# Shorter list of final waits, a first tile loaded in two halves, and two warming products fewer in a fused attention and feed-forward kernel

## The chip, the cores and the metric

The kernel runs on one core of one Trainium2 chip. The metric is the time of one execution on the device in microseconds (us), taken as the median over runs. Before the change three runs took 705.91, 705.12 and 705.55 us, so the median is 705.55 us.

The core's engines are TensorE (PE, matrix products), VectorE (DVE), ScalarE (ACT), GpSimd (POOL) and SyncE (SP). Each runs its own list of instructions in order, and semaphores make one list wait for another. In this kernel SP issues nearly all DMA transfers, POOL those that add to their destination.

## The reference, cut to what matters

All tensors are bf16. x is 2048 rows of 1024, wqkv is 1024 × 3072, wo 1024 × 1024, w_gate and w_up 1024 × 3584, w_down 3584 × 1024.

```
xn  = (x - mean(x)) / sqrt(var(x) + 1e-5)              # each row of 1024
q, k, v = split(xn @ wqkv)                             # 32 heads of 32
phi(t)  = where(t > 0, t + 1, exp(t)) + 1e-6
kv  = sum over rows of phi(k)^T v,  z = sum over rows of phi(k)   # per head
o   = (phi(q) @ kv) / (phi(q) . z + 1e-6)
s   = o @ wo
g   = silu( (silu(xn @ w_gate) * (xn @ w_up)) @ w_down )
out = x + s * g
```

The attention is linear: it needs no products between rows, but k and v of all 2048 rows must be there before any o can be made.

## The kernel before, in words

**A plan, then five lists.** The kernel first writes down every piece of work as an operation of a `Plan` (lines 31 to 216): its engine, what it reads and writes, an assumed duration, and, for a DMA, its size and semaphore. `op` (line 49) derives from reads and writes which operations must come before it. `schedule` (line 92) then fixes the order on each engine. It goes backwards through the operations and gives each a due time, the earliest that its followers allow, held to within `CLAMP` = 1000 us of PE's work so far, less its `urgent` (line 99). Then it goes forward: for PE it takes the first ready product in the order of writing, within a window of 10 operations; for any other engine it takes the ready operation with the smallest rank, due time less `boost` (line 144). The table `BOOST` (line 1730) gives boosts by the operation's number in the order of writing, so a number means another operation as soon as one is added or removed ahead of it. `emit` (line 187) turns the order into five lists of instructions and puts in a wait wherever an engine doesn't yet know that a predecessor is done. A chip executes the lists as they are; the plan's assumed times only set the order.

**What is computed when.** x is worked on in 16 tiles of 128 rows. `ln_tile` (line 734) normalises a tile: two `bn_stats` of half the columns each (lines 739 and 740), their aggregate (745), the variance plus epsilon (746), the power −0.5 on POOL (749), and for tiles 0 and 1 two `tensor_scalar` on DVE for half the columns each (755). `t_tile` (line 779) transposes the first four tiles on PE (line 237 is where the transposes are recorded) and copies them out of PSUM on ACT (804); later tiles are transposed by DMA. k and v of tiles 0 and 1 are made by plain products (`p_piece`, line 864), those of the other tiles by a scheme that needs seven products for a 2 × 2 block of tiles in place of eight. After that come q, gate, up, attention output and down projections, all in the seven-product scheme, in part nested twice, with intermediate results in DRAM scratch. Line 230 is where every matrix product is recorded, line 358 every ACT operation, line 368 every DVE addition or product of two tensors, line 371 every DMA of SP, line 222 every wait that needs an instruction of its own.

**The start.** PE first runs `NWARM` = 13 products of 128 × 512 on a zeroed tile (line 483 to 485), which nobody reads. Meanwhile SP issues the loads of lines 925 to 928. Each x tile is one DMA of 256 KB (`x_load`, 720), and the weights of k and v are eight blocks of 512 KB (`wkv_load`, 725). A block is called (w, j, k) here: w = 0 for k's weights and 1 for v's, j the half of the columns, k the half of the rows. k's products of tiles 0 and 1 need (0,0,0), (0,0,1), (0,1,0) and (0,1,1): the two with equal j make one result, four products for each block and tile. All loads of this list get `urgent` = 60 − 2n by their place in it (line 932), whatever they got before; the normalising products of tiles 0 and 1 get up to 100 (758), which their predecessors inherit through the due times. With its boosts SP issues x0, (0,1,0), x1, (0,0,0), (0,0,1), (0,1,1), and after those the rest. In `ln_tile` tile 1's first statistics also follow tile 0's variance and its second ones tile 0's second normalising product (741 to 744).

In the old table the entries 29 to 34 are the loads x0, x1, (0,1,0), (0,1,1), (0,0,0) and (0,0,1), and 41 and 42 are tile 0's two statistics.

**The end.** The output is made in four groups of 512 rows. The first three copy x to the output beforehand and add to it with POOL's accumulating DMAs (1593). The last group adds x on DVE and stores with plain DMAs of SP (1599): eight pieces of 128 × 512, except that the last piece is cut in three columns' ranges (`PIECES`, 1449), so there are ten stores, each with a semaphore of its own. After its last instruction SP waits for every DMA semaphore's final value, one by one in the order in which the semaphores were made (lines 1742 to 1744); consecutive waits are packed by the compiler where they can be.

Of the kernel before, what the change touches and what calls it, by code (L numbers as in the profile page):

```python
# [12 lines left out]
BF16 = mybir.dt.bfloat16  # L13
FP16 = mybir.dt.float16
KB = 1024
# [222 lines left out]
    return last  # L238


def build_kernel(nc, A_x, A_wqkv, A_wo, B_w_gate, B_w_up, B_w_down, out, WINDOW=10, NWARM=13, NPE=4, LEAD=16.0, CLAMP=1000.0, AHEAD=4.0):
    S, D, FF = 2048, 1024, 3584
    NT, KT, NG, NPAIR = 16, 8, 8, 14
    EPS_LN, EPS_PHI = 1e-5, 1e-6
# [1 line left out]
    xf = A_x.rearrange("b s d -> (b s) d")  # L246
# [7 lines left out]
    with ExitStack() as es:  # L254
# [20 lines left out]
        def named(*key):  # L275
            return Region([key])
# [11 lines left out]
        stats = TM.at(15 * KB + 256, 192, F32).rearrange("p (i h n) -> p i h n", h=2, n=6)  # L288
# [38 lines left out]
        def sem(name):  # L327
            return es.enter_context(nc.semaphore(name))

        esem = {k: sem("s_" + k) for k in Plan.ENGS}  # L330
        semn = {}

        def dsem(name):
            if name not in semn:
                semn[name] = sem("d_" + name)
            return semn[name]

        PL = Plan(WINDOW, LEAD, CLAMP, AHEAD)
# [18 lines left out]
        def act(reads, writes, o, i, func, src="ps", **kw):  # L357
            op = PL.op("act", reads, writes, lambda h: h.activation(o, i, func, **kw),  # L358
                       nel(o) / 1200.0 + (0.055 if src == "ps" else 0.095))
            if func in (ACT.Exp, ACT.Silu):  # L360
                op.tab = func
            return op

        def dve(reads, writes, fn, n, rate=0.96):
            return PL.op("dve", reads, writes, fn, n / (rate * 1000.0) + 0.07)
# [4 lines left out]
        def dma(reads, writes, o, i, s, nbytes, cow=None, after=None):  # L370
            return PL.op("sp", reads, writes, lambda h: h.dma_start(o, i), 0.08, sem=s, nbytes=nbytes, cow=cow,
                         after=after)
# [37 lines left out]
        def pool(reads, writes, fn, busy=0.3):  # L410
            return PL.op("pool", reads, writes, fn, busy)
# [308 lines left out]
        def x_load(i):  # L720
            s = x_ring.take()
            xslot[i] = s
            dma([], [s.r], s.ap(), xf[i * 128:(i + 1) * 128, :], dsem("x%d" % s.k), 256 * KB).urgent = 10.0

        def wkv_load(w, j, k):
            ap, r = kvblock(w, KB_OF[k, j])
# [5 lines left out]
        first_var = []  # L732

        def ln_tile(i):
            j = i % 4
            s = xslot[i]
            xa = s.ap()
            sA, sB, mvr, ver, rsr, nmr = (named(n, j) for n in ("sA", "sB", "mv", "ve", "rs", "nm"))
            o0 = dve([s.r], [sA], lambda h: h.bn_stats(stats[:, j, 0, :], xa[:, 0:512]), 512)
            o1 = dve([s.r], [sB], lambda h: h.bn_stats(stats[:, j, 1, :], xa[:, 512:1024]), 512)  # L740
            if i == 1:
                for o, p in ((o0, first_var[0]), (o1, first_var[-1])):
                    o.preds.add(p)
                    p.succs.append(o)
            dve([sA, sB, TM.reg(15 * KB + 256, 192)], [mvr], lambda h: h.bn_aggr(mv[:, j, :], stats[:, j, :, :]), 60)
            o0 = dve([mvr], [ver], lambda h: h.tensor_scalar(veps[:, j, :], mv[:, j, 1:2], EPS_LN, None, ALU.add), 60)
            if i == 0:
                first_var.append(o0)
            pool([ver, nh_r], [rsr], lambda h: h.tensor_tensor(rstd[:, j, :], veps[:, j, :], neg_half[:, :], ALU.pow), 0.56)
            o = xn_ring.take()  # L750
            xnslot[i] = o
            oa = o.ap(FP16)
            if i < 2:
                for c in (0, 512):
                    n = dve([s.r, mvr, rsr], [o.sub(2 * c, KB).r], lambda h, c=c: h.tensor_scalar(
                        oa[:, c:c + 512], xa[:, c:c + 512], mv[:, j, 0:1], rstd[:, j, :], ALU.subtract, ALU.mult),
                        512, 2.6)
                    n.urgent = 100.0 - c / 25 - 40 * i
                    if i == 0:
                        first_var.append(n)  # L760
            else:
                dve([mvr, rsr], [nmr], lambda h: h.scalar_tensor_tensor(
                    nmean[:, j, :], mv[:, j, 0:1], -1.0, rstd[:, j, :], ALU.mult, ALU.mult), 60)
                act([s.r, nmr, rsr], [o.r], oa, xa, ACT.Identity, "sb", bias=nmean[:, j, :],
                    scale=rstd[:, j, :]).busy = 1.13
# [159 lines left out]
        for n, (fn, args) in enumerate(((x_load, (0,)), (x_load, (1,)), (wkv_load, (0, 1, 0)), (wkv_load, (0, 1, 1)),  # L925
# [5 lines left out]
            for o in PL.ops[k:]:  # L931
                o.urgent = 60.0 - 2 * n
        ln_tile(0)
        t_tile(0)
        ln_tile(1)
        t_tile(1)
        p_piece(0, 0, 1)
# [3 lines left out]
        x_load(5)  # L941
        p_piece(1, 0, 0)
        ln_tile(2)
        p_piece(0, 1, 1)
        t_tile(2)
# [693 lines left out]
        sp = {}  # L1639
# [81 lines left out]
        for g, c in enumerate(G):  # L1721
# [5 lines left out]
        feed(None)  # L1727
        flush()

        BOOST = {1: 5058, 29: 18306, 30: 754, 31: 18202, 32: 872, 33: 880, 34: 881, 37: 3, 39: 68, 41: -2586,  # L1730
# [7 lines left out]
        for k, v in BOOST.items():  # L1738
            PL.ops[k].boost = v
        PL.schedule()  # L1740
        prog = PL.emit(esem)
        for s in semn.values():
            if id(s) in PL.count:
                prog["sp"].append(("w", s, PL.count[id(s)]))

        @block.tensor
        def _(h):
# [19 lines left out]
def bass_recurrent_scan__linear_attn_block__swiglu_ffn__prompt_kernel(  # L1767
    nc: bass.Bass,
    A_x: bass.AP,
    A_wqkv: bass.AP,  # L1770
    A_wo: bass.AP,
    B_x: bass.AP,
    B_w_gate: bass.AP,
    B_w_up: bass.AP,
    B_w_down: bass.AP,
    out: bass.AP,
):
    build_kernel(nc, A_x, A_wqkv, A_wo, B_w_gate, B_w_up, B_w_down, out)
# [28 lines left out]
```

## Time and profile before

| | |
|---|---|
| median of three runs | 705.55 us (705.12 to 705.91) |
| the profiled execution | 704.51 us |
| its span, first to last instruction | 702.7 us |
| mean granted TensorE clock | 0.998 |
| PE busy | 694.8 us, 4436 products and transposes |
| DVE, ACT, POOL busy | 610.7, 424.7, 68.4 us |
| DMA | 103.68 MB, mean 148 GB/s |

The profile is of one execution. Its times count from the first instruction. The execution took 1.81 us more than its span, which lies around the instructions. A busy time is a sum of an engine's durations; PE's weight loads (PEld) go beside its products. In a timeline or chain a row gives start, length, engine, line of the kernel, operation, what is written and read, shapes, the number of instructions taken together, and in brackets the idle time of the engine before it and what ended it. `SPq` is SP's queue of instructions, whose DMA issues aren't counted as busy.

### The profile page before, as it was taken

How to read it: one execution, taken by the hardware profiler on the slowest of the kernel's cores; microseconds unless marked ns; L12 is line 12 of the kernel's file. 1: busy time of each engine (PE TensorE's matmuls, PEld its weight loads, DVE VectorE, ACT ScalarE, POOL GpSimd, SP SyncE). 2: the span in 40 equal slices, each digit the busy share in tenths (PEclk: the TensorE clock that was granted, in tenths of full speed). 3: DMA queues.
4: the chain of work that ended last, by engine and by line, in shares of the span. 5: the costliest groups of instructions: out<-in, count | busy, mean ns of one | idle time of the engine just before them, and what ended most of it. 6: DMA issues, size and time to landing. Idle time of an engine off the chain costs nothing.

```text
span 702.7 us, 11996 instructions
## 1 busy us (share of the span) xinstructions
PE 694.8 (99%) x4436; PEld 421.4 (60%) x4436; DVE 610.7 (87%) x1391; ACT 424.7 (60%) x848; POOL 68.4 (10%) x87
## 2 busy tenths in 40 slices
PE   8999999999999999999999999999999999999996
PEld 3544445555555566666666666666665448687784
DVE  6999998667999799898999999888879998768685
ACT  4877645867978967868866567775763113232222
POOL 2111000001100011020110110001101211111010
PEclk9999999999999999999999999999999999999999
DMA  9434213126612376584670486766627875666672
GB/s 313 106 83 106 54 60 121 61 90 145 155 61 69 117 195 169 174 236 101 166 194 1 106 242 198 242 218 165 165 81 225 192 182 176 155 165 156 207 180 69
DMA packets 96107, 103.68 MB, mean 148 GB/s; under 512 B 18256, under 2 KB 91344, under 8 KB 95952
## 3 DMA queue, kind: packets, MB, share of 16 engines
q1 hardware_dynamic: 84976, 92.43, 41.9%
q0 software_dynamic: 11072, 10.49, 11.9%
q8 instruction: 35, 0.57, 0.3%
q14 instruction: 24, 0.20, 0.1%
HBM read 65.54 MB, written 37.36 MB: 146 GB/s over the span
## 4 chain that ended last, share of the span: by engine, by line
PE 99%; ACT 0%; POOL 0%; DVE 0%; issue 0%; POOLq 0%
PE ps L230 99%; PE ps L237 0%; ACT X L358 0%; DVE W L368 0%; POOL TM L415 0%; ACT W L358 0%; POOL TM L414 0%; POOLq L1792 0%
## 5 line engine op out<-in xcount | busy, mean ns | idle before, releaser
L358 ACT ACTIVATE TM<-ps 128x512 f32<-128x512 f32 (+2 forms) x341 | 169.0, 528 | 50.5 <-PE ps L230 45.6
L368 DVE TENSOR_TENSOR ps<-ps,TM 128x256 f32<-128x256 f32 (+1 forms) x322 | 157.7, 509 | 40.2 <-PE ps L230 35.8
L230 PE MATMUL ps<-X,W 128*128 128x512 f16 (+1 forms) x896 | 190.4, 340 | 0.0
L230 PE MATMUL ps<-P,W 128*128 128x512 f16 (+1 forms) x896 | 188.9, 338 | 0.0
L358 ACT ACTIVATE H<-ps 128x512 f16<-128x512 f32 (+1 forms) x181 | 106.3, 601 | 55.9 <-PE ps L230 54.9
L230 PEld LDWEIGHTS ps<-X,W 128*128 128x128 f16 (+1 forms) x896 | 87.5, 98 | 59.5 <-DVE W L368 0.2
L230 PEld LDWEIGHTS ps<-P,W 128*128 128x128 f16 (+1 forms) x896 | 87.6, 98 | 58.4 <-DVE ps L368 0.2
L358 ACT ACTIVATE ps<-ps 128x256 f32<-128x256 f32 (+2 forms) x149 | 63.5, 426 | 72.5 <-PE ps L230 70.9
L230 PE MATMUL ps<-H,X 128*128 128x512 bf16 (+4 forms) x556 | 104.8, 336 | 0.5 <-ACT X L358 0.5
L368 DVE TENSOR_TENSOR H<-H 128x1024 f16<-128x1024 f16 (+5 forms) x150 | 87.1, 598 | 10.6 <-ACT H L358 8.4
L368 DVE TENSOR_TENSOR W<-W 128x256 f16<-128x256 bf16 (+6 forms) x256 | 89.1, 388 | 5.1 <-PE ps L230 2.9
L230 PE MATMUL ps<-W 128*128 128x256 f16 x512 | 90.0, 273 | 0.0
L368 DVE TENSOR_TENSOR TM<-ps,TM 128x512 f32<-128x512 f32 x99 | 67.8, 686 | 12.5 <-PE ps L230 11.5
L230 PEld LDWEIGHTS ps<-H,X 128*128 128x128 f16 x556 | 52.8, 98 | 41.6 <-ACT X L358 0.6
L375 POOL DMA_DIRECT2D h_scratch<-H x28 | 33.7, 1283 | 437.4 <-DVE H L368 197.0
L230 PEld LDWEIGHTS ps<-W 128*128 128x128 f16 (+1 forms) x512 | 50.0, 98 | 27.3 <-ACT TM L358 0.6
L230 PE MATMUL ps<-H,W 128*128 128x512 f16 (+2 forms) x280 | 63.6, 358 | 0.0
L230 PE MATMUL ps<-H 128*128 128x256 f16 (+4 forms) x432 | 60.9, 273 | 0.0
L230 PE MATMUL ps<-W,H 128*128 128x256 f16 (+1 forms) x314 | 53.5, 305 | 0.0
L358 ACT ACTIVATE H<-TM 128x512 f16<-128x512 f32 x61 | 38.3, 631 | 15.6 <-DVE TM L368 15.0
L230 PEld LDWEIGHTS ps<-H 128*128 128x128 f16 (+1 forms) x432 | 38.3, 98 | 14.6 <-ACT H L358 0.2
L368 DVE TENSOR_TENSOR H<-ps,TM 128x512 f16<-128x512 f32 (+1 forms) x59 | 40.3, 685 | 2.7 <-PE ps L230 2.5
(92 smaller groups left out, 552.1 us busy)
## 6 DMA issues: line engine op xcount, KB each, us to landing
h_scratch<-H SPq DMA_DIRECT2D x70, 256.0 KB, 3.2
X<-h_scratch SPq DMA_DIRECT2D x15, 896.0 KB, 5.2
W<-in_B_w_gate_dram SPq DMA_DIRECT2D x7, 1024.0 KB, 5.4
W<-in_B_w_up_dram SPq DMA_DIRECT2D x7, 1024.0 KB, 6.1
h_scratch<-H POOLq DMA_DIRECT2D x28, 256.0 KB, 5.7
H<-in_B_w_down_dram SPq DMA_DIRECT2D x8, 896.0 KB, 6.7
W<-in_A_x_dram SPq DMA_DIRECT2D x16, 256.0 KB, 3.1
H<-in_A_wqkv_dram SPq DMA_DIRECT2D x8, 512.0 KB, 7.9
```

Of the source, the lines that this page charges most:

```text
L230: last = h.matmul(o, l, r, start=st, stop=sp, skip_group_check=True)
L358: op = PL.op("act", reads, writes, lambda h: h.activation(o, i, func, **kw), nel(o) / 1200.0 + (0.055 if src == "ps" else 0.095))
L368: return dve(reads, writes, lambda h: h.tensor_tensor(o, a, b, op), nel(o), 1.92 if fast else 0.96)
L375: return PL.op("pool", reads, writes, lambda h: h.dma_start(o, i, accum_op=ALU.add), 1.0, sem=s, nbytes=2 * nbytes)
```

## The change

Four things are edited. The number of warming products goes from 13 to 11. Tile 0's load is cut into two halves of 512 columns each, 128 KB; SP issues the first and ACT the second, with a new semaphore, and the statistics of a half then depend on that half alone; tile 0's second statistics follow its first. Both statistics of tile 1 now follow tile 0's second normalising product. And the final waits are only for DMAs that have no successor in the plan, with the last value of each such semaphore. The table of boosts is replaced; since two warming operations go and one load is added, an operation after the loads has a number one lower than before.

```diff
-def build_kernel(..., WINDOW=10, NWARM=13, ...):
+def build_kernel(..., WINDOW=10, NWARM=11, ...):
...
         def x_load(i):
             s = x_ring.take()
             xslot[i] = s
-            dma([], [s.r], s.ap(), xf[i * 128:(i + 1) * 128, :], dsem("x%d" % s.k), 256 * KB).urgent = 10.0
+            rows = xf[i * 128:(i + 1) * 128, :]
+            if i == 0:
+                dma([], [s.sub(0, KB).r], s.ap(BF16, 0, KB), rows[:, 0:512], dsem("x0"), 128 * KB)
+                PL.op("act", [], [s.sub(KB, KB).r], lambda h: h.dma_start(s.ap(BF16, KB, KB), rows[:, 512:1024]), 0.5,
+                      sem=dsem("xh"), nbytes=128 * KB)
+                return
+            dma([], [s.r], s.ap(), rows, dsem("x%d" % s.k), 256 * KB).urgent = 10.0
...
-            o0 = dve([s.r], [sA], lambda h: h.bn_stats(stats[:, j, 0, :], xa[:, 0:512]), 512)
-            o1 = dve([s.r], [sB], lambda h: h.bn_stats(stats[:, j, 1, :], xa[:, 512:1024]), 512)
+            o0 = dve([s.sub(0, KB).r], [sA], lambda h: h.bn_stats(stats[:, j, 0, :], xa[:, 0:512]), 512)
+            o1 = dve([s.sub(KB, KB).r], [sB], lambda h: h.bn_stats(stats[:, j, 1, :], xa[:, 512:1024]), 512)
+            if i == 0:
+                o1.preds.add(o0)
+                o0.succs.append(o1)
             if i == 1:
-                for o, p in ((o0, first_var[0]), (o1, first_var[-1])):
+                for o, p in ((o0, first_var[-1]), (o1, first_var[-1])):
...
-        BOOST = {1: 5058, 29: 18306, 30: 754, 31: 18202, 32: 872, 33: 880, 34: 881, 37: 3, 39: 68, 41: -2586,
-                 42: 6519, 46: 4544, 49: 3050, 51: 459, 60: 181, 78: 407, 80: 3, 104: 60, 117: 570, 123: 103, 142: 3,
+        BOOST = {1: 724, 27: 73363, 32: 9572, 33: 881, 44: 20, 45: 85, 46: 120, 48: 1646, 71: 80, 99: 150, 110: 224,
+                 112: 20, 122: 3053, 123: 20, 143: 6, 151: 8, 154: 8, 258: 20, 950: 3, 954: 60, 971: 8, 1931: 20,
...
         prog = PL.emit(esem)
-        for s in semn.values():
-            if id(s) in PL.count:
-                prog["sp"].append(("w", s, PL.count[id(s)]))
+        ends = {}
+        for o in PL.order:
+            if o.sem is not None and not o.succs:
+                ends.pop(id(o.sem), None)
+                ends[id(o.sem)] = o.ev
+        for s, _, val, _ in ends.values():
+            prog["sp"].append(("w", s, val))
```

More of the change, by code (lines that the diff above doesn't have):

```diff
@@ L238, in _tr_group, with build_kernel @@
     return last
-def build_kernel(nc, A_x, A_wqkv, A_wo, B_w_gate, B_w_up, B_w_down, out, WINDOW=10, NWARM=13, NPE=4, LEAD=16.0, CLAMP=1000.0, AHEAD=4.0):
+def build_kernel(nc, A_x, A_wqkv, A_wo, B_w_gate, B_w_up, B_w_down, out, WINDOW=10, NWARM=11, NPE=4, LEAD=16.0, CLAMP=1000.0, AHEAD=4.0):
     S, D, FF = 2048, 1024, 3584
```

10 rows, old and new, of the table BOOST are left out of this document.

## Prediction

> **What bounds the kernel now.** I read the page first: the span and how much of it TensorE (PE) works.
>
> ```profile
> span 702.7 us, 11996 instructions
> PE 694.8 (99%) x4436; PEld 421.4 (60%) x4436; DVE 610.7 (87%) x1391; ACT 424.7 (60%) x848; POOL 68.4 (10%) x87
> ```
>
> PE is busy for all but 7.9 us. A mean does not say where those lie, so the second view is the busy time by stretches (columns: stretch and length, then busy us and count of PE, PE weight loads, DVE, ACT, POOL, then granted clock, DMA share, GB/s).
>
> ```profile
> 1.40:7.00 5.60, 5.57 (x16) 2.09 (x17) 2.87 (x7) 0.68 (x1) 2.92 (x14) 1.00 0.93 303
> 7.00:11.10 4.10, 3.63 (x29) 1.84 (x26) 1.81 (x6) 1.20 (x3) 0.55 (x1) 1.00 1.10 363
> 11.10:100.00 88.90, 88.90 (x496) 43.71 (x495) 85.95 (x213) 64.31 (x101) 10.17 (x14) 1.00 0.42 107
> 100.00:600.00 500.00, 500.00 (x3157) 302.17 (x3155) 445.72 (x1017) 331.56 (x689) 41.11 (x37) 1.00 0.55 149
> 600.00:696.80 96.80, 96.74 (x748) 71.58 (x745) 73.53 (x148) 26.07 (x57) 12.99 (x16) 1.00 0.61 166
> ```
>
> From 11.1 to 696.8 us PE is busy 685.64 of 685.70 us: the middle is bound by PE alone and has nothing to give. The diff removes no product there, so a new order of the side engines can only keep this or spoil it. What can be won lies before 11.1 us and after 696.8 us.
>
> The third view is SyncE's (SP's) own instructions after 696 us: its stores of the output (durations, first and last start), how long the last store takes to land (KB, us), and the event-semaphore instructions of line 222, before and after 700.5 us.
>
> ```profile
> L371 SPq DMA_DIRECT2D out_dram<-W x4: 332/431/600, 696.0 to 697.9; - x4
> ```
> ```profile
> out_dram<-W SPq DMA_DIRECT2D x2, 32.0 KB, 1.5
> ```
> ```profile
> L222 SPq EVENT_SEMAPHORE  x34: 17/28/28, 698.4 to 700.4; - x34
> ...
> L222 SPq EVENT_SEMAPHORE  x25: 27/28/28, 700.8 to 702.2; - x25
> ```
>
> The last store is issued at 697.9 and lands 1.5 us later, at 699.4. Yet SP goes on until 702.2, through 59 instructions (34 and 25) that wait for the semaphores of all DMAs. Each takes 28 ns but they start 0.06 us apart (34 in 2.0 us), with one pause of 0.4 us between 700.4 and 700.8. From 699.4 on nothing is outstanding: SP only walks through a list. **The end is bound by the length of that list, not by the last store.**
>
> The fourth view is the timeline of the start.
>
> ```profile
> 0.80 1.28 ACT L358 ACT_TABLE_LOAD   x1 [0.80 <-PEq L1792]
> ...
> 1.26 0.42 SPq L371 DMA_DIRECT2D H<-in_A_wqkv_dram  x1
> ...
> 1.43 5.59 PE L230 MATMUL ps<-TM 128*128 128x512 f16 x13 [1.43 <-POOL TM L415]
> ...
> 1.73 0.51 SPq L371 DMA_DIRECT2D W<-in_A_x_dram  x1
> ...
> 2.27 2.29 SPq L371 DMA_DIRECT2D H<-in_A_wqkv_dram  x4
> ...
> 3.37 0.69 DVE L739 BATCH_NORM_STATS2 TM<-W 128x6 f32<-128x512 bf16 x1 [2.18 <-DMA W<-in_A_x_dram]
> ...
> 5.78 0.73 DVE L755 TENSOR_SCALAR W<-W,mv,rstd 128x512 f16<-128x512 bf16 x2 [0.69 <-POOL rstd L749]
> ...
> 6.43 0.69 DVE L739 BATCH_NORM_STATS2 TM<-W 128x6 f32<-128x512 bf16 x1
> ...
> 6.85 0.61 PE L237 MATMUL ps<-TM,W 128*128 128x128 f16 x8
> ...
> 7.93 2.80 PE L230 MATMUL ps<-H,X 128*128 128x512 bf16 x12 [0.47 <-ACT X L358]
> ...
> 8.82 0.73 DVE L755 TENSOR_SCALAR W<-W,mv,rstd 128x512 f16<-128x512 bf16 x2 [0.67 <-POOL rstd L749]
> ...
> 11.11 1.29 DVE L368 TENSOR_TENSOR H<-H 128x1024 f16<-128x1024 bf16 x2 [1.56 <-DMA H<-in_A_wqkv_dram]
> ...
> 11.13 8.81 PE L230 MATMUL ps<-H,X 128*128 128x512 bf16 x40
> ```
>
> The first half of tile 0 is normalised by about 6.15 (5.78 and half of 0.73), but its transposes start at 6.85, when the 13th warming product is through: here the warming is the bound, by 0.7 us. And at 11.11 a DVE operation, at 11.13 PE, start as the fourth weight block arrives: **there the bound is DMA arrival**, which the row of 7.0 to 11.1 us supports with 363 GB/s.
>
> **The change part by part.** *End waits.* The list of 59 instructions shrinks to the semaphores of DMAs that no later operation follows. By the code these are the ten stores of the last row group, each with a semaphore of its own; accumulating stores are followed by the next writer of their buffer. Ten waits are at most ten instructions, 0.6 us from 698.35, so SP stands ready by 699.0 and waits for the last store at 699.4. Behind the last wait the old kernel needed 0.45 us to its end (702.25 to 702.7); the new one then ends at about 699.4 + 0.05 + 0.45 = 699.9. The saving is 2.8 us. Bounds: 2.4 if the pause of 0.4 us comes back, 2.9 if the last wait is passed at once. What is late next is the last store itself, issued and landing as before.
>
> *Eleven products.* 13 took 5.42 us (1.43 to 6.85), 0.42 each, so two fewer give 0.83: PE is free at 6.0. The transposes can then start at 6.0 to 6.2, set by whichever is later, warming or normalising: 0.65 to 0.83 us earlier than now. Whether that reaches the end is decided by the weights, below.
>
> *Two halves.* No row of this trace shows a DMA issued by ACT. An issue of x1 took SP 0.51 us; on ACT it comes ahead of the table load of 1.28 us, which carries the line of the first ACTIVATE, and both are done by about 2.6, long before ACT's first work near 6.5. So it costs nothing there. If instead the table load goes first, the second half is issued at 2.08, 1.28 late, and lands near 4.6; its statistics, now possible from 4.06 (3.37 + 0.69), would start 0.55 late and the transposes near 6.7, about where they are now. At best half the bytes at 363 GB/s land 0.36 us sooner. I take no gain and no loss: the warming holds the transposes until 6.0 anyway.
>
> *Statistics of tile 1 behind both normalisings of tile 0.* In the trace they already come behind them (6.43 after 5.78 + 0.73 with its overlap). DVE has only tile 1's own chain behind the wait. Nothing, as long as tile 1 arrives later than 6.5; the next part says that it does.
>
> *The order of the loads.* This is the part the short list does not name. SP takes loads by due time less boost. The old boosts gave x0, (0,1,0), x1, (0,0,0), (0,0,1), (0,1,1). With two products fewer and one load more, every later index is one lower; the new entries at 27, 32 and 33 are x0's first half, (0,0,0) and (0,0,1). Due times are clamped to within about 1000, so 73363 and 9572 decide outright, and 881 nearly so; of the others x1 is due before the blocks, since it inherits the urgency of the normalising. The new order is x0, (0,0,0), (0,0,1), x1, (0,1,0), (0,1,1). How long a place in that queue takes is shown by the issues of the second, third and fourth load (KB, us to landing):
>
> ```profile
> H<-in_A_wqkv_dram SPq DMA_DIRECT2D x1, 512.0 KB, 4.2
> ```
> ```profile
> W<-in_A_x_dram SPq DMA_DIRECT2D x1, 256.0 KB, 4.4
> ```
> ```profile
> H<-in_A_wqkv_dram SPq DMA_DIRECT2D x1, 512.0 KB, 5.8
> ```
>
> With the issue times, 768 KB have landed at 1.26 + 4.2 = 5.5, 1024 KB at 1.73 + 4.4 = 6.1, 1536 KB at 2.27 + 5.8 = 8.1, and 2560 KB at 11.1, which puts 2048 KB at 9.6. The sum of bytes stays, so the new kernel has (0,0,0) at 5.5, (0,0,1) at about 7.1, **x1 at 8.1 in place of 6.1**, (0,1,0) at 9.6 and (0,1,1) at 11.1. Now PE's work: transposes at 6.1, first products 1.08 later as now (6.85 to 7.93) at 7.2, eight of them at 0.22 (8.81 over 40) to 8.95, with two blocks. Then it waits 0.65 us for (0,1,0), and does four more until 10.5. Tile 1's transposes need its normalising, which begins 2.39 us after its statistics (6.43 to 8.82), at 10.5; the halves are ready at 10.9 and 11.25. They end near 11.45, and the last four products of tile 0 near 12.3. The old kernel has done the same work, eight transposes twice and sixteen products, by 11.13 + 4 × 0.22 = 12.0. So **the 0.7 us won at the transposes are given back as waits for weights and for x1**. Bounds: 0.3 to 0.5 lost if x1 lands as late as its place says and PE holds its last products for it; 0.2 gained if two queues fill the engines sooner. I take a loss of 0.15.
>
> *A shorter warming and the clock.* The 13 products ran at 0.42 us, the later ones of the same shape at 0.22: TensorE ran at half pace until nearly 6.85, though the granted clock stands at 1.00 in the rows above. If it opens at the same moment, near 6.7, the new transposes partly run at half pace: up to 0.45 us, hidden by the 0.65 us that PE then waits for (0,1,0). The Trainium skill, "TensorE: Matmul & The Clock Gate", section "What's actually happening", holds that the gate opens after a free-running window of about 3.4 us in which PE was busy. The trace agrees: its 5.3 us of half pace are more than one such window and less than two. By that rule fewer warming products, followed by PE's waits, can miss a window, which would open the gate near 10.1; an estimate for that is 703.5 us.
>
> *Sum*, against the profiled execution's 704.51 us (span 702.7 and 1.8 around it): −2.8 + 0.15 + 0 = −2.65, or 701.9. The median of the runs shown, 705.55, is 1.04 above that execution; with the same difference I forecast **702.9 us**.
>
> **The rivals.** *First, the start gains as well.* Then x1 lands well before its place and PE does not wait at 9 us: up to 0.6 us more, 702.1. Against it is the arrival of (0,1,1) at 11.1 in both orders, with too little work ready before it. *Second, the new order leaves a hole in the middle.* Some seventy boosts change. For it: DVE is busy 85.95 of 88.90 us before 100 us, so an operation that goes first there delays another. Against it: PE waited nowhere for 685 us. One late buffer costs about 1 us (an operation of DVE or two): 703.9. *Third, the gate stays half shut.* Place: PE's work after 6.1. In the trace half pace lasted from 1.43 to about 6.7, 5.3 us, without an idle stretch. If the idle moments after the eleventh product start that anew, it lasts until 11.4: half of the work in 5.3 − 0.6 us (the wait for ACT) is lost, 2.35, less about 1.1 hidden in the waits near 9 and 11, so 1.2: 704.1. If the wait near 11 starts it once more, it lasts until 16.3, costs (10.2 − 0.6) / 2 − 1.1 = 3.7 and gives 706.6, slower than before. That side begins where the loss passes 2.65, with an opening later than about 6.1 + 0.6 + 2 × 3.75 = 14.2 us. Against it: the old kernel's transposes end near 7.3 (eight, a quarter of 0.22 each), PE then waits 0.6 us until 7.93, and that did not bring half pace back. *Fourth, the end does not shrink:* more DMAs than the ten count as last. With half the list left SP ends at 698.35 + 1.9 + 0.45 = 700.7, 2.0 sooner, which gives 703.7; with all of it, 705.7.
>
> **How the numbers follow.** Forecast 0.62; start gains 0.13; hole in the middle 0.12; gate late once 0.06, twice 0.03; end not shrunk 0.04. 0.2% of 705.55 is 1.4 us, about what a measurement of this kernel can tell from no change: faster means below 704.14, slower above 706.96. All of the first two count as faster, three quarters of the hole, two thirds of the gate late once and half and more of the fourth: 0.91 faster, 0.06 same, 0.03 slower. The range goes from 702.0 (start gains) to 704.1 (a hole, or a gate late once), and the runs shown differ by 0.4 either way, which lies within it around the forecast.
>
> **What would show it.** Right: at most ten event-semaphore instructions on SP after the last store, and an end 0.5 us after it lands; transposes near 6.1; a wait of PE near 9 us and one near 11, and PE dense from about 11.4. Wrong: PE idle between 12 and 696 us (second rival), products of 0.42 us after 7.5 (third), or sixteen products of tile 0 done well before 12.0 (first).

## The result, and the profile after

The kernel before ran in 705.25 us (median of six runs, 704.91 to 705.91), the changed one in 702.86 us (six runs, 702.68 to 703.69). The ratio is 0.9968, with a 95% interval of 0.9956 to 0.998. The forecast was 702.9 us. The total holds. Of the sum's two terms that were not zero one, the final waits, was right to a tenth; the other, the start's loss, was more than four times too small; and in the profiled execution a cost came on top that the sum did not have.

That execution took 703.48 us, 0.62 above the median of its kernel, where the one of before lay 0.74 below its own. So the two profiles differ by 1.0 us only, the medians by 2.4. The page after shows the span and PE:

```profile
span 701.7 us, 11926 instructions
PE 692.4 (99%) x4413; PEld 420.9 (60%) x4434; DVE 610.7 (87%) x1391; ACT 424.4 (60%) x848; POOL 67.9 (10%) x87
```

Here 4413 of PE's products were recorded; 4434 weight loads stand beside them, so some 20 records are missing, and PE's sums below are short by about as much. The stretches of the changed kernel (columns as before):

```profile
7.00:12.30 5.30, 3.53 (x25) 1.68 (x25) 2.89 (x7) 1.11 (x3) 0.55 (x1) 1.00 1.08 361
12.30:100.00 87.70, 87.23 (x483) 43.27 (x490) 83.94 (x210) 63.77 (x100) 9.67 (x14) 1.00 0.44 104
100.00:600.00 500.00, 499.53 (x3144) 301.69 (x3151) 445.83 (x1018) 331.72 (x688) 40.51 (x36) 1.00 0.55 149
```

From 12.3 us on PE is as dense as it was: the gaps of 0.47 us stand where there are 7 records fewer than weight loads. In the 5.3 us before, it works 3.53. The timeline of the start shows why (start, length, engine, and in brackets the idle time before and what ended it):

```profile
0.81 0.40 ACTq L726 DMA_DIRECT2D W<-in_A_x_dram  x1
...
1.43 3.94 PE L230 MATMUL ps<-TM 128*128 128x512 f16 x11 [1.43 <-POOL TM L415]
2.27 0.50 SPq L371 DMA_DIRECT2D W<-in_A_x_dram  x1
...
3.56 0.69 DVE L745 BATCH_NORM_STATS2 TM<-W 128x6 f32<-128x512 bf16 x1 [2.36 <-DMA W<-in_A_x_dram]
...
6.58 0.72 PE L237 MATMUL ps<-TM,W 128*128 128x128 f16 x8 [1.20 <-DVE W L764]
7.67 1.04 PE L230 MATMUL ps<-H,X 128*128 128x512 bf16 x4 [0.37 <-ACT X L358]
8.67 0.69 DVE L745 BATCH_NORM_STATS2 TM<-W 128x6 f32<-128x512 bf16 x1 [1.82 <-DMA W<-in_A_x_dram]
10.11 1.90 PE L230 MATMUL ps<-H,X 128*128 128x512 bf16 x8 [1.41 <-DMA H<-in_A_wqkv_dram]
11.06 0.73 DVE L764 TENSOR_SCALAR W<-W,mv,rstd 128x512 f16<-128x512 bf16 x2 [0.67 <-POOL rstd L758]
...
11.85 0.61 PE L237 MATMUL ps<-TM,W 128*128 128x128 f16 x8
...
12.30 1.03 PE L230 MATMUL ps<-H,X 128*128 128x512 bf16 x4
```

The warming ends at 5.37 and now PE waits 1.2 us for DVE: tile 0's normalising has become the bound of the transposes, at 6.58, and no longer the warming. After four products PE waits 1.41 us for block (0,1,0); tile 1's statistics begin at 8.67, where they began at 6.43 before; its transposes begin at 11.85; and tile 0's last four products begin at 12.30.

The end shows SP's issues of the output (durations in ns: least, median, most; first and last start), its last semaphore instructions, and how long the last stores took to land:

```profile
L371 SPq DMA_DIRECT2D out_dram<-W x5: 332/430/1292, 696.4 to 699.7; - x5
```
```profile
L222 SPq EVENT_SEMAPHORE  x5: 17/28/28, 700.2 to 701.3; - x5
```
```profile
out_dram<-W SPq DMA_DIRECT2D x2, 32.0 KB, 1.5
```

59 instructions have become five. The last one starts at 701.3, when the last store (issued at 699.7, 1.5 us to landing) is there, and the span ends about 0.5 us later. Nothing is walked through after the landing. But one issue took 1292 ns, where the longest took 600 before.

### The profile page after: what moved, and what is told of

Read it like the earlier page. It is cut to its first block, busy times and chain, and to the rows that moved or that the text cites. A ratio compares the mean times of both kernels' runs of the same rounds, so it can differ in the third digit from the quotient of the medians.

```text
span 701.7 us, 11926 instructions
## 1 busy us (share of the span) xinstructions
PE 692.4 (99%) x4413; PEld 420.9 (60%) x4434; DVE 610.7 (87%) x1391; ACT 424.4 (60%) x848; POOL 67.9 (10%) x87
## 4 chain that ended last, share of the span: by engine, by line
PE 97%; DMA 1%; DVE 0%; ACT 0%; SPq 0%; issue 0%
PE ps L230 97%; DMA H<-in_A_wqkv_dram 1%; SPq L371 0%; PE ps L237 0%; DVE H L844 0%; ACT TM L358 0%; ACT H L358 0%; DVE TM L843 0%; ACT ps L358 0%; DVE W L368 0%; ACT W L358 0%; DVE nmean L771 0%
## 5 line engine op out<-in xcount | busy, mean ns | idle before, releaser
L230 PE MATMUL ps<-H,X 128*128 128x512 bf16 (+4 forms) x545 | 102.6, 335 | 2.4 <-DMA H<-in_A_wqkv_dram 1.4
```

What stands on the lines that cost most here:

```text
L230: last = h.matmul(o, l, r, start=st, stop=sp, skip_group_check=True)
```

## The experiments

Each kernel ran five times or more, beside the kernel before, and each has a profile. Medians of such small changes overlap, so two readings of the profile are compared as well. They split a time at two points that every kernel has: the landing of the fourth block of k's weights, (0,1,1) in both orders, and the end of the last two DVE additions, which make the last piece of output. Between them lies nearly all the work; after the second lies the end. In the kernel before, and then in the changed one, these additions are

```profile
697.08 0.48 DVE L368 TENSOR_TENSOR W<-W 128x128 f16<-128x128 f16 x2 [0.22 <-ACT W L358]
```
```profile
698.24 0.49 DVE L368 TENSOR_TENSOR W<-W 128x128 f16<-128x128 f16 x2 [0.22 <-ACT W L358]
```

With the landing at 11.09 the first gives 697.56 − 11.09 = 686.47 us of work. In the changed kernel the block is issued at about 3.3 and lands 8.3 later, at 11.57:

```profile
H<-in_A_wqkv_dram SPq DMA_DIRECT2D x1, 512.0 KB, 8.3
```

which gives 698.73 − 11.57 = 687.16: **0.69 more**. Over the kernels with the old loads the reading repeats to 0.04 us. The end takes 702.7 − 697.56 = 5.1 us before, 701.7 − 698.73 = 3.0 after.

### The new final waits alone: end_only

The theory was the prediction's: the end gives about 2.8, the start next to nothing. The rival was that the start gave part of it, or took part of it back.

```diff
(kernel before)
-        for s in semn.values():
-            if id(s) in PL.count:
-                prog["sp"].append(("w", s, PL.count[id(s)]))
+        ends = {}
+        for o in PL.order:
+            if o.sem is not None and not o.succs:
+                ends.pop(id(o.sem), None)
+                ends[id(o.sem)] = o.ev
+        for s, _, val, _ in ends.values():
+            prog["sp"].append(("w", s, val))
```

> The kernel before with the new final waits alone; plan and every other instruction are as before. My theory (the end gives about 2.8 us and the start takes some back): 2.8 us less than before, about 702.4 us, that is below the changed kernel. Rival (the end gives only what the changed kernel's median shows, 2.4 us, and the start changes nothing): 702.85 us. Second rival (SP is late with the last store, so the list was partly hidden): 2.2 us less, 703.1 us.

Measured: 702.49 us (702.11 to 703.24) against 705.18 before in the same session, ratio 0.9958 [0.9945, 0.9971]. The one edit gives 2.7 us, no less than the whole change. Its profile, SP's instructions and then DVE's last additions:

```profile
L371 SPq DMA_DIRECT2D out_dram<-W x5: 332/430/1122, 695.8 to 699.0; - x5
```
```profile
L222 SPq EVENT_SEMAPHORE  x5: 17/28/28, 699.5 to 700.6; - x5
```
```profile
697.72 0.49 DVE L368 TENSOR_TENSOR W<-W 128x128 f16<-128x128 f16 x2 [0.22 <-ACT W L358]
```

The list of the emitted instructions is the old one up to the final waits, and the work from the landing (11.70) to the additions takes 698.21 − 11.70 = 686.51, as before. One thing is not as before: an issue of 1122 ns.

### The changed kernel with the old final waits: start_only

```diff
(changed kernel)
-        ends = {}
-        for o in PL.order:
-            if o.sem is not None and not o.succs:
-                ends.pop(id(o.sem), None)
-                ends[id(o.sem)] = o.ev
-        for s, _, val, _ in ends.values():
-            prog["sp"].append(("w", s, val))
+        for s in semn.values():
+            if id(s) in PL.count:
+                prog["sp"].append(("w", s, PL.count[id(s)]))
```

> The changed kernel with the old list of final waits: halves, eleven warming products, the new order of tile 1's statistics and the new boosts without the new end. My theory: slower than before by what the start loses, 0.4 to 1.2 us, 705.7 to 706.5 us, with PE idle for about 1.6 us before the products that need block (0,1,0). Rival (the start changes nothing): 705.3 us. Rival (the start gains): below 704.8 us.

Measured: 706.22 us (twelve runs, 704.55 to 708.38) against 705.18, ratio 1.0015 [1.0005, 1.0026]. All edits of the start together lose 1.0 us, between 0.4 and 1.8. The runs lie far apart: nine from 704.55 to 706.55, three from 708.13 to 708.38. The three have a mean granted clock of 0.996, the nine of 0.997 to 0.999. The profiled execution, 708.15 us, is one of the three. Its semaphore instructions at the end, and PE's timeline of the start:

```profile
L222 SPq EVENT_SEMAPHORE  x59: 27/28/28, 702.0 to 706.0; - x59
```
```profile
7.80 1.04 PE L230 MATMUL ps<-H,X 128*128 128x512 bf16 x4 [0.37 <-ACT X L358]
11.12 3.50 PE L230 MATMUL ps<-H,X 128*128 128x512 bf16 x8 [2.28 <-DMA H<-in_A_wqkv_dram]
14.46 0.61 PE L237 MATMUL ps<-TM,W 128*128 128x128 f16 x8
14.90 7.07 PE L230 MATMUL ps<-H,X 128*128 128x512 bf16 x32
```

Eight products take 3.50 us here, 1.90 in the changed kernel's profile, although the 32 after them take 0.22 each. The granted clock of that stretch (the third number from the end of the row) says the same, and DVE's last additions give the price:

```profile
10.98:14.39 3.41, 3.27 (x8) 1.19 (x9) 2.71 (x7) 0.00 (x0) 0.55 (x1) 0.50 1.10 355
```
```profile
700.85 0.48 DVE L368 TENSOR_TENSOR W<-W 128x128 f16<-128x128 f16 x2 [0.22 <-ACT W L358]
```

Half pace came back after a wait of 2.28 us, which is **the third rival's mechanism in an execution**. Its price is 3.50 − 1.90 = 1.6 us; the work from the landing (12.56) to the end of the additions (701.33) is 688.77, 1.6 above the changed kernel's 687.16. The changed kernel has the same start, so it is open to this as well; its six runs, up to 703.69 us, show no such step. The Trainium skill, "TensorE: Matmul & The Clock Gate", section "What's actually happening", puts the return to half pace after at least one idle window of some 3.4 us; here PE had no such pause, only 2.28 us, with little work (four products) in the 3.4 us before 11.1. In this execution a shorter pause was enough.

The 59 instructions run from 702.0 to 706.0; the last store lands at 703.1, so some 2.9 us of the list lie behind it. From the last additions to the end of the span, less the duration of the issue of the 64 KB store, it is 5.13 − 0.60 = 4.53 us before and 5.08 − 0.51 = 4.57 here, but 3.02 − 1.29 = 1.73 after and 2.85 − 1.12 = 1.73 in end_only: the list was worth 2.8 us in both starts.

### The products of the block that comes first: pe_swap

PE's list in the changed kernel has the four products of (0,1,0) ahead of those of (0,0,1), although (0,0,1) lands 2.2 us sooner. This kernel exchanges them.

```diff
(changed kernel)
         PL.schedule()
+        # the four products of (0,0,1) right before the four of (0,1,0)
+        o = PL.ops[75]
+        PL.order.remove(o)
+        PL.order.insert(PL.order.index(PL.ops[62]), o)
```

> The changed kernel with one change in PE's list: the four products of block (0,0,1) go ahead of the four of block (0,1,0); all loads stay where they are. If PE's order alone makes the wait at 8.5 us, the wait shrinks to 0.7 us and the kernel gains 0.35 us, until tile 1's transposes (its normalising ends near 11.8 us) hold PE: 702.5 us. If the late second tile is the only bound, nothing is gained: 702.86 us.

Measured: 703.22 us (701.61 to 704.5) against 705.18, ratio 0.9968 [0.9956, 0.998]. No gain. PE's timeline shows what is then in the way, the second fence how long the fourth block took, and the third DVE's last additions:

```profile
11.14 1.04 PE L230 MATMUL ps<-H,X 128*128 128x512 bf16 x4 [1.11 <-DMA H<-in_A_wqkv_dram]
12.58 0.72 PE L237 MATMUL ps<-TM,W 128*128 128x128 f16 x8 [0.40 <-DVE W L764]
13.13 7.07 PE L230 MATMUL ps<-H,X 128*128 128x512 bf16 x32
```
```profile
H<-in_A_wqkv_dram SPq DMA_DIRECT2D x1, 512.0 KB, 9.3
```
```profile
699.19 0.49 DVE L368 TENSOR_TENSOR W<-W 128x128 f16<-128x128 f16 x2 [0.22 <-ACT W L358]
```

Now PE has eight products behind it when (0,1,0) comes, as the prediction had assumed; it does four more and waits 0.40 us for DVE's normalising of tile 1. From the landing (12.58) to the end of the additions (699.67) it is 687.09 us, nearly what the changed kernel takes. So PE's list alone does not make the loss: with it out of the way, the late x1 holds PE almost as long. In the changed kernel the two end together, PE's eight products by 11.85 and tile 1's normalising at 11.06 + 0.73 = 11.79; what the list alone would cost no run shows.

### The first loads and products in the old order: old_start_order, early_loads_old

Both keep the halves, the eleven products, the order of the statistics and the new waits, and put the first loads of SP (x1, (0,1,0)) and PE's first products back in the old order. The first of them also puts a block of v's weights ahead of tile 2 of x, as in the kernel before.

```diff
(changed kernel; ahead(n, m) moves operation n right before m in PL.order)
         PL.schedule()
+        for n, m in ((30, 32), (29, 32), (38, 34), (62, 74)):    # old_start_order
+        for n, m in ((30, 32), (29, 32), (62, 74)):              # early_loads_old
+            ahead(n, m)
```

> The changed kernel with the loads of x1 and of the six weight blocks in the order of the kernel before, and PE's first three groups of products in the old order too; halves, eleven warming products, final waits and all later work as in the changed kernel. If the new order of loads is what the start pays for, PE reaches the products of (0,1,1) near 11.2 us and the kernel gains 0.7 to 1.1 us on the changed one: 701.8 to 702.2 us. If the halves or the shorter warming are to blame, it gains less than 0.3 us: 702.6 to 702.9 us.

> The changed kernel with x1 and the four k blocks in the old order of loads and PE's two first groups of products swapped to fit; unlike the earlier try, the third x tile keeps the place that the changed kernel gives it, ahead of v's first blocks. Theory (the new order of loads is what the start pays for): no wait of PE near 18 us, PE dense from 11.3 us, and 0.6 us or more below the changed kernel: about 702.2 us. Rival (the halves and the shorter warming are to blame): at or above 702.86 us.

old_start_order: 703.22 us (702.95 to 703.72), ratio 0.9969 [0.9957, 0.9981]. It missed what was expected, and its PE timeline shows that the loss moved to another place:

```profile
11.32 7.09 PE L230 MATMUL ps<-H,X 128*128 128x512 bf16 x32
19.25 0.62 PE L237 MATMUL ps<-TM,W 128*128 128x128 f16 x8 [0.84 <-ACT W L358]
```

PE is dense from 11.32 on, but at 19.25 the transposes of tile 2 wait 0.84 us. In this kernel x2 comes behind a block of v, and the likely reading is that the rest of the changed plan does not go with that load's place. From the landing (11.27) to the additions the work is 687.62. early_loads_old leaves it where the change has it: 702.06 us (701.77 to 703.51) against 704.97, ratio 0.9967 [0.9954, 0.9979]. Its fourth block (DVE waits for it, 12.25) and its last additions:

```profile
12.25 0.69 DVE L368 TENSOR_TENSOR H<-H 128x1024 f16<-128x1024 bf16 x1 [1.21 <-DMA H<-in_A_wqkv_dram]
```
```profile
698.23 0.48 DVE L368 TENSOR_TENSOR W<-W 128x128 f16<-128x128 f16 x2 [0.22 <-ACT W L358]
```

With the landing at 12.22, 698.71 − 12.22 = 686.49: with the first loads in the old order the work takes what it took before, with all other edits of the start in place. So these others are worth nothing, together, and the order of the first loads, with PE's products to fit, accounts for all of the 0.69. No run moves x1 alone; that x1 matters in it is read from pe_swap.

### One edit of the start at a time: end_halves, end_warm11, end_new_loads

Each is end_only with one thing more.

```diff
(end_only, after PL.schedule(); op 29 is the load of x0, op 42 tile 0's second statistics)
+        # end_halves
+        PL.ops[29].fn = lambda h: h.dma_start(s0.ap(BF16, 0, KB), xf[0:128, 0:512])
+        xh = PL.op("act", [], [], lambda h: h.dma_start(s0.ap(BF16, KB, KB), xf[0:128, 512:1024]), 0.5,
+                   sem=dsem("xh"), nbytes=128 * KB)
+        PL.ops[42].preds.add(xh)
...
+        # end_warm11
+        for o in PL.ops[23:25]:
+            PL.order.remove(o)
...
+        # end_new_loads: loads (0,0,0), (0,0,1) ahead of x1 and (0,1,0); PE's products of (0,0,0) first
+        for n, m in ((33, 31), (34, 31), (30, 31), (75, 63), (35, 39)):
+            ahead(n, m)
```

> The kernel before with the new final waits and x's first tile in two halves, the second issued by ACT; every engine's order is otherwise as in end_only. Theory: the first DVE statistics start 0.1 to 0.2 us later than with one load, since both halves share the same DMA engines and come as twice as many packets; PE's products are held by the weight blocks, so the time equals end_only's 702.5 us within 0.2 us. Rival (two queues fill the engines sooner): first statistics before 3.2 us and the time 0.2 to 0.4 us below end_only.

> The kernel before with the new final waits and without its last two warming products; every engine's order is otherwise as in end_only. Theory: the transposes start up to 0.5 us earlier when the clock is still at half pace, but the products wait for block (0,0,1) near 9.6 to 10.3 us either way, so the time equals end_only's 702.5 us within 0.2 us. Rival (the clock gate): with PE idle after eleven products the half pace lasts longer or returns in some runs, and the median rises by 0.5 us or more, above 703.0 us.

> The kernel before with the new final waits and, of all the rest, only the changed kernel's order of the first loads (x0, (0,0,0), (0,0,1), x1, (0,1,0), (0,1,1), third x tile) with PE's products of (0,0,0) ahead of those of (0,1,0) to fit; whole x0, thirteen warming products, everything later as in end_only. Theory (the order of the loads is the whole loss of the start): PE waits for (0,1,0) near 10 us and then for tile 1, the last DVE addition comes about 687.1 us after block (0,1,1) lands in place of 686.5, and the time is 0.4 to 0.8 us above end_only: 702.9 to 703.3 us. Rival (the loss needs the halves or the shorter warming too): as end_only, 702.5 us.

Measured against 704.97 in both sessions: end_halves 702.41 (702.09 to 702.97), ratio 0.9967 [0.9954, 0.9979]; end_warm11 702.30 (702.1 to 702.53), 0.9965 [0.9951, 0.9978]; end_new_loads 702.30 (702.06 to 703.23), 0.9965 [0.9952, 0.9977]. By the medians none of the three does anything, and for the last one that is not what was expected. Of end_halves the first statistics, the wait for the fourth block and the last additions:

```profile
3.70 0.69 DVE L739 BATCH_NORM_STATS2 TM<-W 128x6 f32<-128x512 bf16 x1 [2.50 <-DMA W<-in_A_x_dram]
```
```profile
11.77 1.29 DVE L368 TENSOR_TENSOR H<-H 128x1024 f16<-128x1024 bf16 x2 [1.30 <-DMA H<-in_A_wqkv_dram]
```
```profile
697.75 0.48 DVE L368 TENSOR_TENSOR W<-W 128x128 f16<-128x128 f16 x2 [0.22 <-ACT W L358]
```

The first statistics start at 3.70, 0.33 later than in the kernel before (3.37). Much of that is chance: in the six profiles with a whole x0 they start at 3.37 to 3.67, in the six with halves at 3.56 to 3.85, 0.2 later on the average. The work takes 698.23 − 11.75 = 686.48: nothing gained and nothing lost. The same two rows of end_warm11,

```profile
11.44 1.29 DVE L368 TENSOR_TENSOR H<-H 128x1024 f16<-128x1024 bf16 x2 [1.39 <-DMA H<-in_A_wqkv_dram]
```
```profile
697.42 0.49 DVE L368 TENSOR_TENSOR W<-W 128x128 f16<-128x128 f16 x2 [0.22 <-ACT W L358]
```

give 697.91 − 11.42 = 686.49. For end_new_loads, PE's and DVE's timelines and the load of the fourth block:

```profile
9.20 1.90 PE L230 MATMUL ps<-H,X 128*128 128x512 bf16 x8 [0.47 <-DMA H<-in_A_wqkv_dram]
10.94 0.61 PE L237 MATMUL ps<-TM,W 128*128 128x128 f16 x8
11.38 8.80 PE L230 MATMUL ps<-H,X 128*128 128x512 bf16 x40
```
```profile
697.32 0.48 DVE L368 TENSOR_TENSOR W<-W 128x128 f16<-128x128 f16 x2 [0.22 <-ACT W L358]
```
```profile
H<-in_A_wqkv_dram SPq DMA_DIRECT2D x1, 512.0 KB, 7.4
```

The fourth block landed at 10.65, sooner than in any other of the profiles, yet PE's run of 40 products starts at 11.38, 0.73 after it, where with the old loads it starts with it (before: landing 11.09, products 11.13). The work is 697.80 − 10.65 = 687.15, 0.68 more than before, with nothing edited at the start but the order of the loads and PE's products to fit. The median does not show it; the landing itself differs by more, between 10.65 and 12.58 over the kernels' profiles (last section).

### Tile 1 first: end_tile1_first

If tile 1's readiness is what PE needs with the new loads, it might gain with the old loads to transpose tile 1, and make its first four products, before PE waits for the later blocks.

```diff
(end_only)
         PL.schedule()
+        for n, m in ((58, 76), (59, 76), (61, 76), (69, 64)):
+            ahead(n, m)
```

> The kernel before with the new final waits, and in PE's list tile 1's transposes ahead of the products of block (0,0,1) and tile 1's first four products ahead of those of block (0,1,1), so that PE has work while those blocks are on their way. Loads and warming as before. Theory (the start is bound by the arrival of weights, with the order of PE's list deciding what is done meanwhile): PE's waits near 9.5 and 11 us go, and the kernel is 0.3 to 0.6 us below end_only: 701.9 to 702.2 us. Rival (tile 1 is ready too late to be of use): no gain, 702.5 us.

Measured: 702.39 us (701.51 to 702.94), ratio 0.9965 [0.9952, 0.9977], no gain over end_only. Its PE timeline from 11 us on:

```profile
10.79 2.75 PE L230 MATMUL ps<-H,X 128*128 128x512 bf16 x12
13.86 1.90 PE L230 MATMUL ps<-H,X 128*128 128x512 bf16 x8 [0.31 <-ACT TM L358]
```

What PE did ahead of the fourth block is in part paid back at 13.86, where it waits 0.31 us for ACT, which copies out of PSUM. Its last additions,

```profile
697.24 0.49 DVE L368 TENSOR_TENSOR W<-W 128x128 f16<-128x128 f16 x2 [0.22 <-ACT W L358]
```

end at 697.73, and from the landing at 11.24 the work takes 686.49, as with the old list of PE: nothing is left of the gain.

### Moving an instruction fetch: end_pe_shift

The issue of the 64 KB store took 600 ns before, 1292 after, 1122 in end_only, 813 in end_warm11, 333 in end_tile1_first, though the store is the same. In the changed kernel the transfers of 697.0 to 699.8 us hold one that is none of the kernel's (columns: packets, MB, share of 16 engines):

```profile
q8 instruction: 1, 0.02, 3.9%
```

It is one packet of 16 KB that takes 0.039 × 16 × 2.8 = 1.75 us, from 697.10 to 698.84, and the issue that began at 697.92 ends at 699.21, 0.37 us later. Queue q8 fetches PE's instructions, 35 times in the span, one packet for every 256 instructions or so. The theory: such a fetch holds up the issue. end_pe_shift is end_warm11 with six warming products each cut in four of 128 columns, so that PE's list is 18 products longer (36 instructions with weight loads, not 32 as the expectation has it) and the fetch comes sooner by some 1.5 us.

```diff
(end_warm11)
         PL.schedule()
...
+        for n in range(6):
+            PL.ops[12 + n].fn = partial(_mm_group, [
+                (ps[n][:, c:c + 128], ident[:, :], wz[:, c:c + 128], True, True) for c in range(0, 512, 128)])
```

> The kernel before with the new final waits, eleven warming products, and the first six of these cut into four of 128 columns each, so that PE's list is 32 instructions longer than in end_warm11 at the same place of the end. Theory (the store of 64 KB is issued late since a 16 KB instruction fetch of PE, a packet of queue q8, runs through the DMA engines just then): the fetch comes about 1.5 us earlier, near 695 us, the issue of the 64 KB store takes 0.33 us instead of 0.75 to 1.3, and the tail from the last DVE addition to the end is 2.1 us instead of 2.5 to 3.0; the time is 0.3 us below end_warm11, about 702.0 us. Rival (the late issue has to do with the store itself): the issue stays above 0.7 us.

Measured: 702.11 us (701.75 to 702.61) against 704.97, ratio 0.9958 [0.9945, 0.9972]. Its issue of the 64 KB store, and before that of end_warm11 the four issues that include it:

```profile
L371 SPq DMA_DIRECT2D out_dram<-W x4: 332/436/813, 696.3 to 698.4; - x4
```
```profile
L371 SPq DMA_DIRECT2D out_dram<-W x1: 333/333/333, 698.0 to 698.0; - x1
```

The fetch, in the stretch from 695.1 to 696.7 us,

```profile
q8 instruction: 1, 0.02, 5.6%
```

takes 0.056 × 16 × 1.6 = 1.4 us, from 695.24 to 696.66. It is over before the issue at 698.0, and the issue takes 333 ns in place of 813. The other profiles agree. In ten of the twelve a fetch is under way when this store's issue begins, and the issue ends 0.31 to 0.38 us after the fetch; in end_tile1_first and here the fetch is over, and the issue takes 333 ns. So the delay by the fetch is shown. Not every issue is held up, though: in the changed kernel the 128 KB store before it, issued at 697.15 within the same fetch, took 332 ns. What tells the two apart is open. The 0.5 us that the shift gives do not show against end_warm11's median (702.30).

## Why the prediction was right

**End waits: right.** Ten waits at most, an end 0.5 us after the last store has landed, 2.8 us. It is five instructions, an end 0.5 us after the landing (701.27 to 701.75), and 2.8 us to a tenth, with the old start (end_only) and with the new one (start_only against the changed kernel). That lies within the bounds of 2.4 and 2.9; the pause of 0.4 us did not come back.

**Eleven products: right, by the cover.** The step said that the transposes could start at 6.0 to 6.2, 0.65 to 0.83 sooner. They started at 6.58, 0.27 sooner, because the normalising, not the warming, had become the later of the two. The normalising began at 6.11 in place of 5.78: the first statistics started 0.19 later, and the second ones, made to follow the first, 0.73 after them in place of 0.61. Alone the edit is worth nothing (end_warm11), as the weights' arrival decides.

**Two halves: right on the sum, for another reason.** ACT's issue does come ahead of its table load (0.81), as assumed, and the engine loses nothing. But the halves don't land sooner: the first statistics start at 3.56 in place of 3.37, 3.70 in end_halves. Over all profiles halves are 0.2 us later; why is not shown. It is a small loss, hidden by the same cover.

**Statistics of tile 1: right.** early_loads_old has this edit with x1 early, and its work takes 686.49 us.

**The order of the loads: the term that was mis-sized.** The order on SP came as read from the boosts, and x1 landed at 8.57 (2.27 and 6.3 us), forecast 8.1. The step that failed is "eight of them at 0.22 to 8.95, with two blocks". PE's list has the products of (0,1,0) second, so PE did four products, to 8.5 or so, and the next eight after 10.07. With those done near 11.9 and tile 1's transposes behind them, its last four began at 12.30; the forecast had them near 11.45 and ended them at 12.3. The row at 12.30 thus stands 0.85 later than the step said. Of this 0.47 is the later landing of the fourth block (11.57 in place of 11.1), and 0.38 the step itself. The forecast's own rows already lost 0.3 (12.3 against 12.0), of which it took half; 0.3 and 0.38 make 0.68, and 0.69 was measured. pe_swap shows that PE's list alone is not it: with the forecast's own order on PE, x1's landing (9.63, 2.95 before the fourth block, where the forecast had 3.0) and the normalising behind it hold PE until 13.13, 0.55 after that block where the forecast had 0.35. The loss is 0.6 to 0.7 from the landing of the fourth block on, in place of 0.15, and above the upper bound of 0.5.

**Why the total still fits.** In the profiled executions the difference is made up as follows: −2.80 for the list, +0.69 for the longer issue of the 64 KB store, +0.48 for the later fourth block (11.57 against 11.09), +0.69 for the order of the loads: −0.94. The spans differ by 0.95 (702.70 against 701.75), the executions by 1.03 (703.48 against 704.51). In the medians it is −2.39, 0.26 short of the forecast's −2.65. But the forecast took its 2.65 off 705.55, the median of the three runs shown, and over six runs the median before is 705.25, 0.30 lower. The two errors cancel, and that the total is right to 0.04 us is luck. List and order of the loads alone would give −2.1; that and −2.39 both lie in the interval of the ratio (1.4 to 3.1 us saved), and no run here measures what makes up the rest. The landing and the issue of the 64 KB store change from one execution to the next, and the forecast had no term for either.

**The rivals.** The first (start gains) is out: PE waits as forecast. The second (a hole in the middle) is not in the trace. The third (half pace comes back) was taken for 0.09; it did not happen in the changed kernel's profile, where the eight products after a wait of 1.41 us take 1.90, and it did in the profile of start_only, whose wait was 2.28. That start_only's two other runs above 708 us have the same cause is argued from their clock of 0.996 alone. The fourth (the end does not shrink) is out. The prediction let half pace open "at the same moment, near 6.7"; it opens near 4.3 in the changed kernel (eleven products in 3.94 us, where 13 took 5.42). The Trainium skill, "TensorE: Matmul & The Clock Gate", section "What's actually happening", has the window run free of the kernel's start, and that agrees: with the first product at 1.43 or 1.44 in all, half pace ends at 4.2 in start_only, 5.2 in end_only, 6.7 before and after 7.1 in end_warm11.

**What is best.** The new waits with the old loads are as fast as the changed kernel or faster: end_only 702.49, end_warm11 702.30, early_loads_old 702.06, end_pe_shift 702.11 against 702.86. By their intervals they can't be told apart, among themselves or from it. The medians point the same way as the profiles: leaving out old_start_order with its wait at 19.25, the six kernels with the new waits and the old loads lie at 702.06 to 702.49, the three with the new loads at 702.30, 702.86 and 703.22.

## What to carry to other kernels

Look at what the issuing engine does after its last store has landed; here 59 instructions that waited for DMAs, nearly all long landed, were 2.8 us, and a list of the last DMAs alone gives them back whatever the rest of the kernel does. At a start that is bound by DMA, try a small load that heads a long chain (x1: statistics, normalising, transposes) ahead of large ones that are only multiplied; here the order with x1 behind one weight block took 0.7 us less work than the one with x1 behind two. A faster first step did nothing, since the last arrival was what PE waited for. And where executions differ by more than the effect, measure from an event that they share (here the landing of the last block): the readings 686.47 to 686.51 (seven kernels with the old loads) and 687.09 to 687.16 (three with the new ones) separate what no median did. Two kernels lie outside for reasons of their own: start_only by its half pace and old_start_order by its wait at 19.25.

## What the runs showed of the hardware

**The landing of the first blocks varies by 1.9 us.** The fourth block landed at 11.09 before, 11.57 after, 11.70 in end_only, 12.56 in start_only, 12.58 in pe_swap, 12.31 in end_pe_shift, 10.65 in end_new_loads, with the same bytes ahead of it. In the traces the semaphore of a load is raised 16 times, and the load is complete with the last. For the fourth block the middle ones of the 16 come at 10.0 to 10.8 in every profile, the last 0.5 to 2.4 us after them. In pe_swap a single one is late, 2.1 to 2.2 us behind the other 15 in every load from the second weight block to the fourth, so what is lost early is not made up; in end_only many come late. Why was not found.

**An instruction fetch delays an issue.** At the end of the kernels one 16 KB fetch of PE's instructions took 0.9 to 1.75 us, and the issue of the 64 KB store, where it began within the fetch, ended 0.3 to 0.4 us after it and took up to 1390 ns (pe_swap) in place of 333. The store issued before it within the same fetch was not delayed (332 ns in the changed kernel).

**Half pace after a short wait.** 2.28 us without work brought it back in one execution (granted clock 0.50 from 10.98 to 14.39 in start_only), 1.41 did not in another. At the start the granted clock doesn't tell: the row of 1.40 to 7.00 us before has 1.00, while its products take 0.42 us in place of 0.22.
